# Loading the first head group's q and k in memory order, with 32-row score products, in a fused attention and mixture-of-experts kernel

## The chip, the cores and the metric

The kernel runs on one core of a Trainium2 chip. The metric is the device time of one execution in microseconds (us). Before the change the median of three runs is 844.26 us (844.2 to 844.76). The execution that the profiler recorded took 843.34 us, with a span of 841.6 us from its first to its last instruction.

## The reference

Attention over 8 batches, 12 heads, 448 positions and 64 dimensions per head, with capped scores, followed by a mixture of 8 experts in which tokens are assigned in order of their gate logits. All numbers are float32.

```
scores = q @ k.T / sqrt(64)
scores = cap * tanh(scores / cap)
attn   = softmax(scores);  x = attn @ v        # x: 3584 tokens of 12*64
logits = x @ w_gate;  each token goes to one of 8 experts, 448 tokens each
out    = relu(x @ w1[e]) @ w2[e]
```

## The kernel before

The attention stage takes about the first 300 us, the experts the rest. Attention works on 24 groups of four heads; a group is called g0, g1 and so on. Queries and keys must have the 64 dimensions on partitions, so each group's q and k are turned by VectorE transposes of 32x32 blocks (function `tr`). For that, `load` brings q and k in as `(k s) d -> s k d` with s=32, in runs of 32 floats (128 bytes). After the transposes a head fills 64 partitions, and two heads stand beside each other in the free dimension.

`qk(g,r)` makes part r of seven of a group's scores: 64 keys of each of the four heads against all 448 queries, as four TensorE products of 64 rows by 64 columns that fill the four quarters of the array, into one PSUM tile of two banks (`two_banks`, three tiles in turn: psM and two ps). ScalarE takes the tile out with a Tanh (L166) and applies Exp to two or three parts at once (L171). `avq` (letter A) multiplies the exponentials with v into a further tile of two banks, psA; `esum` (P, C, S) adds the exponentials up on VectorE. In g1 and later the keys of part r are `r:S:7`, every seventh, so that v can be loaded in long runs; g0 takes its keys in blocks instead, and its v in two tiles `nv0` and `nvh`.

The order on every engine is written out by hand (`manual_schedule`): strings of letters such as `EARLY[0]`, which is g0, say in which order Q (scores), A, transposes of the next group (k, v) and `I` stand. `I6` is `idle(6)`: six products of the identity with itself into psA, whose result nobody reads. Loads are issued by SyncE (SP) in program order, in g0 also by ScalarE's queue; each load from SP waits until the load eight places before it has landed. The table `LD` says which loads stand at the start of which of the first groups ('10' is k of g1, '11' its q, '02' v of g0).

So for g0: k and q come in two halves of eight loads each (L90), two transposes follow each half (L140), three parts of scores follow the first half, four the second.

Of the kernel before, what the change touches and what calls it, by code (L numbers as in the profile page):

```python
# [17 lines left out]
def attention(nc, tc, c1, xp, pM, ep, nl, pT, q, k, v, cap, w_gate, xs, L1, ident, on_logits, on_turn, NDEF, setup, mark, ring):  # L18
# [5 lines left out]
    N=B*NQ  # L24
# [23 lines left out]
    with ExitStack() as ctx:  # L48
# [15 lines left out]
        def load(g,part,lo=0,hi=HG,first=False):  # L64
            if g>=N: return
            b,m=divmod(g,NQ)
            h0=4*m
            if part==2:
                if g:
# [6 lines left out]
                z=nat.tile([128,3,2*HG,D],F32,name="nv0",bufs=1); zh=nat.tile([128,HG,D],F32,name="nvh",bufs=1)  # L76
                nats[g,2]=(z,zh)
                vv=v[b,h0:h0+4,0:384].rearrange("h (j p) d -> j p h d",j=3)
                for j in range(3): nc.sync.dma_start(z[:,j],vv[j])
                for o in range(2):  # L80
                    w=64*(1-o)
                    nc.sync.dma_start(zh[w:w+64],v[b,h0+o:h0+o+3:2,384:448].rearrange("t p d -> p t d"))
                return
            if lo==0: nats[g,part]=nat.tile([128,HG*NB,32],F32,name="kq"[part])
            z=nats[g,part]
            src=(k,q)[part]
            for t in range(2):
                for a in range(2):
                    w=(2*t+a)*32
                    (nc.scalar if first and a else nc.sync).dma_start(z[w:w+32,lo*NB:hi*NB,:],src[b,h0+2*t+lo:h0+2*t+hi,:,a*32:a*32+32].rearrange("h (k s) d -> s (h k) d",s=32))  # L90
        for part in range(2): load(0,part,0,1,True)
        tb=c1.tile([128,1],F32,name="tb")
        nc.scalar.activation(tb,ident[:,0:1],AF.Tanh)
        ips=pT.tile([128,2,512],F32,name="psA",bufs=1)[:,0]
        def idle(n):
            for _ in range(n): nc.tensor.matmul(ips[:,:128],ident,ident,start=True,stop=True)  # L96
# [4 lines left out]
        ones=c2.tile([128,5,32],F32,name="ones")  # L101
# [5 lines left out]
        for o in range(2): nc.gpsimd.memset(ones[:,3+o,24+2*o:25+2*o],1.0)  # L107
# [27 lines left out]
        FIRST=[[(2+h,ones,3,(0,0,h),0) for h in range(2)],[gate(0),gate(1)]+[(2+h,ones,4,(0,1,h),0) for h in range(2)],RB,RE]  # L135
        tks={}; es_t={}; eh={}; misc={}
        def tr(g,part,lo=0,hi=HG):
            if g>=N: return
            if lo==0: tks[g,part]=tp.tile([128,HG,S],F32,name="t"+"kq"[part])
            nc.vector.transpose(tks[g,part].rearrange("p m s -> p (m s)")[:,lo*S:hi*S],nats[g,part][:,lo*NB:hi*NB,:].rearrange("p k d -> p (k d)"))  # L140
        GRP=((0,1,2),(3,4),(5,6)); LOC={r:(gi,n) for gi,rs in enumerate(GRP) for n,r in enumerate(rs)}
        def ev(g,r):
            gi,n=LOC[r]
            return eh[g,gi][:,n]
        ex=lambda g,o,j: ev(g,3*o+j)
        wait=[]; G2=3
        def qk(g,r):
# [3 lines left out]
            if g:  # L151
                for o in range(2):
                    for h in range(2):
                        hp=slice(h*64,h*64+64)
                        nc.tensor.matmul(ps[o*64:o*64+64,h,:S],tks[g,0][hp,o,r:S:7],tks[g,1][hp,o,:],start=True,stop=True)  # L155
            elif r<6:
                o,u=divmod(r,3)
                for h in range(2):
                    hp=slice(h*64,h*64+64)
                    for c in range(2): nc.tensor.matmul(ps[c*64:c*64+64,h,:S],tks[g,0][hp,o,u*128+c*64:u*128+c*64+64],tks[g,1][hp,o,:],start=True,stop=True)  # L160
            else:
                for o in range(2):
                    for h in range(2):
                        hp=slice(h*64,h*64+64); w=64*(1-o)
                        nc.tensor.matmul(ps[w:w+64,h,:S],tks[g,0][hp,o,384:448],tks[g,1][hp,o,:],start=True,stop=True)
# [6 lines left out]
            if g==0 or g==N-1 and gi: act()  # L172
            else: wait.append(act)
        def esum(g,what):
            if not 0<=g<N: return
            if what=='P': es_t[g]=es.tile([128,2,2,S],F32,name="es",bufs=4)
            t=es_t[g]; add=lambda o,x,y: nc.vector.tensor_tensor(o,x,y,op=ALU.add)  # L177
            if what=='P':
                if g: add(t,eh[g,0][:,0:2],eh[g,1])
                else:  # L180
                    for o in range(2): add(t[:,o],ev(g,3*o),ev(g,3*o+1))
            elif what=='C': add(t[:,0],t[:,0],ev(g,2))
            elif what=='r': add(t[:,0],t[:,0],t[:,1])
            elif g: add(t,t,eh[g,2])
            else:
                add(t[:,1],t[:,1],ev(g,5))
                e=ev(g,6)
                for o in range(2):
                    w=slice(64*(1-o),128-64*o)
                    add(t[w,o],t[w,o],e[w])  # L190
        avp={}; pair=[None]
        def avq(g,r):
            if not 0<=g<N: return
            if r==0:
# [3 lines left out]
            if g:  # L198
                z=nats[g,2]
                for o in range(2):  # L200
                    hp=slice(o*64,o*64+64)
                    for h in range(2):
                        nc.tensor.matmul(avp[g,o][h*64:h*64+64,:S],z[hp,r,h,:] if g==N-1 else z[hp,h,r*D:r*D+D],ev(g,r)[hp,h,:],start=r==0,stop=r==6)  # L203
                return
            j,x=(r%3,r//3) if r<6 else (3,1)
            z,zh=nats[g,2]
            for w in range(2):
                o=w^x; hp=slice(w*64,w*64+64)
                for h in range(2):
                    lhs,rhs=(z[hp,j,HG*h+o,:],ex(g,o,j)) if j<3 else (zh[hp,h,:],ev(g,6))  # L210
                    nc.tensor.matmul(avp[g,o][h*64:h*64+64,:S],lhs,rhs[hp,h,:],start=(j==0 and x==0),stop=j==3)
# [128 lines left out]
        for part in range(2): load(0,part,1,2)  # L340
        setup[0]()
        setup[1]()
        for part in range(2): tr(0,part,0,1)
# [5 lines left out]
        for a,t in zip(sr,(s1,capt)): nc.scalar.reg_load(a,t[0:1,0:1].bitcast(I32))  # L349
        bias=c1.tile([128,1],F32,name="bias")  # L350
# [3 lines left out]
        for part in range(2): tr(0,part,1,2)  # L354
        LD={0:['10','11','02','20','21'],1:['12','30','31','g','22'],2:['40','41','32','50','51']}
# [4 lines left out]
        EARLY=["Q0 Q1 k v Q2 I6 Q3 Q4 Q5 Q6 I18","Q0 Q1 A0 P C k S v Q2 A1 A2 Q3 Q4 Q5 Q6 A3 A4 A5 A6","Q0 c Q1 A0 P C k v S r Q2 A1 A2 Q3 Q4 A3 Q5 Q6 A4 A5 A6"]  # L360
# [867 lines left out]
```

## Time and profile before

| what | value |
|---|---|
| median of 3 runs | 844.26 us |
| profiled execution | 843.34 us, span 841.6 us |
| TensorE busy | 829.1 us, 99% |
| VectorE / ScalarE / GpSimd busy | 607.4 / 550.4 / 450.0 us |
| attention | about 0 to 300 us |

A busy TensorE is near its limit all the time, so the table alone does not say where a microsecond can be won. The chain of waits follows the work that ended last back from the end; the timeline shows one engine in order of time, with the idle time before an instruction and what ended it.

### The profile page before, as it was taken

What the parts mean: (1) busy time and instruction counts of PE and PEld (TensorE: products, weight loads), DVE (VectorE), ACT (ScalarE), POOL (GpSimd) and SP (SyncE); (2) the same over time, 40 slices, a digit from 0 to 9 for tenths busy, and PEclk for the clock granted to TensorE, in tenths of its full rate; (3) what the DMA queues carried; (4) which work ended last, traced back from release to release, by engine and by line L of the source; (5) the groups of instructions that cost most, each with busy time, mean ns of one, the idle gap of its engine ahead of it and who ended that gap; (6) DMA issues with size and microseconds to landing.
All of it is one profiled execution on the core that took longest, in us unless ns stands there. A gap on an engine that the chain in (4) does not pass through costs nothing.

```text
span 841.6 us, 17561 instructions
## 1 busy us (share of the span) xinstructions
PE 829.1 (99%) x6053; PEld 640.9 (76%) x6053; DVE 607.4 (72%) x1955; ACT 550.4 (65%) x750; POOL 450.0 (53%) x637
## 2 busy tenths in 40 slices
PE   9999999999999998999999999999999999999997
PEld 6444444444444458889999999999999999999997
DVE  3778899989989877777988888878978973221110
ACT  6999999999999754561664655646636635535521
POOL 8303335344332235573683874856857857846931
PEclk9999999999999999999999999999999999999999
DMA  8999999999993206715716926917918828738501
GB/s 120 140 153 157 157 169 162 160 161 167 156 156 83 44 3 208 252 39 170 232 32 175 316 73 196 341 46 212 315 55 217 293 77 234 252 123 255 186 10 57
DMA packets 330457, 133.70 MB, mean 159 GB/s; under 512 B 251168, under 2 KB 323680, under 8 KB 330368
## 3 DMA queue, kind: packets, MB, share of 16 engines
q1 hardware_dynamic: 320864, 102.27, 55.8%
q0 software_dynamic: 4656, 22.02, 7.6%
q10 hardware_dynamic: 4848, 8.29, 2.9%
q8 instruction: 48, 0.79, 0.4%
q14 instruction: 41, 0.34, 0.1%
HBM read 94.40 MB, written 30.08 MB: 148 GB/s over the span
## 4 chain that ended last, share of the span: by engine, by line
PE 87%; DVE 5%; ACT 4%; issue 3%; POOL 1%; POOLq 0%; DVEq 0%
PE psH L1062 28%; PE psH L1096 26%; PE psA L203 12%; PE ps L155 8%; PE psM L155 4%; ACT e L171 2%; ACT e L166 2%; PE ps L228 2%; PE psA L96 1%; DVE cmpD L614 1%; DVE es L177 1%; PE psX L886 1%; PE psM L228 1%; POOL out_dram L1078 0%; PE psR L809 0%
## 5 line engine op out<-in xcount | busy, mean ns | idle before, releaser
L1096 PE MATMUL psH<-w2h,hh 128*128 128x384 f32 x896 | 232.5, 338 | 0.0
L1096 PE MATMUL psH<-w2l,hh 128*128 128x384 f32 x512 | 166.1, 340 | 0.0
L1096 PEld LDWEIGHTS psH<-w2h,hh 128*128 128x128 f32 x896 | 161.9, 188 | 0.1
L171 ACT ACTIVATE e<-e,bias 128x1792 f32<-128x1792 f32 (+2 forms) x73 | 151.3, 2072 | 0.2
L1062 PE MATMUL psH<-xgh,w1h 128*128 128x448 f32 x384 | 141.5, 369 | 0.3 <-ACT xgh L1022 0.3
L1062 PE MATMUL psH<-xgh,w1l 128*128 128x448 f32 x384 | 140.9, 367 | 0.0
L944 POOL TENSOR_TENSOR w1l<-w1r,w1h 128x768 fp32r<-128x768 f32 x62 | 114.3, 1845 | 40.4 <-ACT w1h L940 35.8
L1062 PE MATMUL psH<-xgl,w1h 128*128 128x448 f32 x384 | 135.6, 366 | 0.0
L203 PE MATMUL psA<-e,nv 64*64 64x448 f32 x1232 | 130.7, 539 | 0.6 <-DVE xT L217 0.5
L944 POOL TENSOR_TENSOR w2l<-w2r,w2h 128x768 fp32r<-128x768 f32 x64 | 118.1, 1848 | 3.2 <-ACT w2h L940 3.2
L166 ACT ACTIVATE e<-ps 128x896 f32<-128x896 f32 x113 | 103.9, 961 | 7.7 <-PE ps L155 3.8
L155 PE MATMUL ps<-tq,tk 64*64 64x448 f32 x864 | 97.1, 539 | 0.1
L203 PEld LDWEIGHTS psA<-e,nv 64*64 64x64 f32 x1232 | 45.4, 133 | 67.8 <-issue 61.0
L1096 PEld LDWEIGHTS psH<-w2l,hh 128*128 128x128 f32 x512 | 95.6, 188 | 0.2
L1071 DVE SCALAR_TENSOR_TENSOR hh<-psH,hh 128x64 fp32r<-128x64 f32 (+1 forms) x128 | 44.0, 385 | 65.2 <-ACT hh L1068 65.1
L1068 ACT ACTIVATE hh<-psH 128x448 fp32r<-128x448 f32 x64 | 34.7, 543 | 83.2 <-PE psH L1062 83.1
L1102 ACT ACTIVATE on<-psH 128x384 f32<-128x384 f32 x48 | 23.6, 491 | 84.6 <-PE psH L1096 79.6
L969 POOL DMA_INDIRECT xg<-xs,idx x32 | 34.7, 1086 | 81.7 <-DVE idx L824 55.4
L1062 PEld LDWEIGHTS psH<-xgh,w1h 128*128 128x128 f32 x384 | 72.3, 188 | 6.0 <-ACT xgh L1022 0.5
L1062 PEld LDWEIGHTS psH<-xgl,w1h 128*128 128x128 f32 x384 | 72.2, 188 | 5.5
L1062 PEld LDWEIGHTS psH<-xgh,w1l 128*128 128x128 f32 x384 | 72.2, 188 | 5.5
L177 DVE TENSOR_TENSOR es<-es,e 128x896 f32<-128x896 f32 (+2 forms) x48 | 72.8, 1517 | 4.3 <-ACT e L171 1.5
(417 smaller groups left out, 1409.3 us busy)
## 6 DMA issues: line engine op xcount, KB each, us to landing
w1r<-in_moe_w_dram SPq DMA_DIRECT2D x128, 192.0 KB, 4.8
w2r<-in_moe_w_dram SPq DMA_DIRECT2D x64, 384.0 KB, 6.1
k<-in_k_dram SPq DMA_DIRECT2D x92, 112.0 KB, 3.6
q<-in_q_dram SPq DMA_DIRECT2D x92, 112.0 KB, 4.1
nv<-in_v_dram SPq DMA_DIRECT2D x88, 112.0 KB, 3.0
xs<-xw SPq DMA_DIRECT2D x72, 112.0 KB, 2.6
xz<-pl ACTq DMA_DIRECT2D x18, 384.0 KB, 3.0
xs<-xn SPq DMA_DIRECT2D x1, 1344.0 KB, 6.6
```

The lines of the kernel that those rows point to most:

```text
L155: nc.tensor.matmul(ps[o*64:o*64+64,h,:S],tks[g,0][hp,o,r:S:7],tks[g,1][hp,o,:],start=True,stop=True)
L166: nc.scalar.activation(ev(g,r),ps[:,:,:S],AF.Tanh,scale=sr[0])
L171: act=lambda: nc.scalar.activation(e,e,AF.Exp,scale=sr[1],bias=bias)
L177: t=es_t[g]; add=lambda o,x,y: nc.vector.tensor_tensor(o,x,y,op=ALU.add)
L203: nc.tensor.matmul(avp[g,o][h*64:h*64+64,:S],z[hp,r,h,:] if g==N-1 else z[hp,h,r*D:r*D+D],ev(g,r)[hp,h,:],start=r==0,stop=r==6)
L228: nc.tensor.matmul(bank[b][q*32:q*32+32,:S],t[:,a,:],rhs,start=n==mine[0],stop=n==mine[-1])
L944: (eng or nc.gpsimd).tensor_tensor(view(l),r,view(h).bitcast(F32),op=ALU.subtract)
L969: g=nc.gpsimd.indirect_dma_start(out=row(j,n),out_offset=None,in_=xs,in_offset=bass.IndirectOffsetOnAxis(ap=res[p][0][:n,j:j+1],axis=0))
L1062: nc.tensor.matmul(ps[:,:C],a[:,c,:],b[:,c,:],start=(m==0),stop=(m==DC*3-1)); m+=1
L1068: nc.scalar.activation(h[:,:C],ps[:,:C],AF.Relu)
L1071: nc.vector.scalar_tensor_tensor(h[:,d:d+b-a],ps[:,a:b],0.0,h[:,a:b].bitcast(F32),op0=ALU.max,op1=ALU.subtract)
L1096: nc.tensor.matmul(ps[:,:HD],h[:,f,a:a+128],spl[p,2,hf,f//2][w][:,f%2,:],start=(m==0),stop=(m==nm-1))
```

## The change

Only g0 changes its way of working; the loads, transposes and sums of other groups keep theirs.

- **Loads** (`load0`). k and q of g0 are read as they lie in memory: partition (head, s) holds 14 consecutive positions with all 64 dimensions, 3584 bytes. There are four loads in place of sixteen: the keys of parts 0 and 1, and q's second half, on SP's queue; q's first half and the remaining keys on ScalarE's.
- **Transposes** (`tr0`). Six in place of four: two of 128 elements per partition for the keys of parts 0 and 1 (written 8 bytes apart), two of 448 for q's halves, two of 320 for the other keys.
- **Scores** (`qk0`). After these transposes a head stands on 32 partitions, and its dimensions in two halves. A score part is the sum of two products of 32 rows by 64 columns. Two parts run together into two tiles, 16 products in all, with parts 1, 4 and 6 (`SWAP`) in the other half of the output partitions, so that eight tiles of the array have work at once. Parts 0 and 1 come in two halves of 224 queries; their fourth tile is psA. The queries are read as `s k` with k innermost: neighbours lie 64 floats (256 bytes) apart.
- **v twice.** g0's v is loaded as that of other groups (nv), and a second time with the head pairs on exchanged partitions (nvx) for the swapped parts; nv0 and nvh are gone.
- **Order.** Fewer idle products at the start (9, not 13), and J8, I10, I8 in place of I6 and I18. Part 2 comes last. A takes g0's parts in the order 1 4 6 0 2 3 5.

```
+        def load0(eng,part,lo,hi,two=False):
+            src=(k,q)[part][0,0:4].rearrange("h (s k) d -> (h s) (k d)",s=32)
+            if two: eng.dma_start(halfs(z)[:,:,lo:hi],halfs(src)[:,:,lo:hi])
+            else: eng.dma_start(z[:,lo:hi],src[:,lo:hi])
...
-        for part in range(2): load(0,part,0,1,True)
-        idle(13)
+        load0(nc.sync,0,0,128,True)
+        load0(nc.scalar,1,0,448)
         nc.sync.dma_start(capt,cap.broadcast_to([128,1]))
+        load0(nc.sync,1,448,896)
+        load0(nc.scalar,0,128,448,True)
+        idle(9,True)
...
+                z=nats[g,3]=nat.tile([128,HG,7*D],F32,name="nvx",bufs=1)
+                    for t in range(2): nc.sync.dma_start(z[64-o*64:128-o*64,t],v[b,h0+2*t+o].rearrange("(p j) d -> p (j d)",j=7))
...
+        def qk0(rs,cuts=(0,14)):
+            tk=tks[0,0].rearrange("p a (j x) -> p j a x",j=7)
+            tq=tks[0,1].rearrange("p m s -> p (m s)").rearrange("p (k a s) -> p a s k",a=2,s=32)
+            for lo,hi in zip(cuts,cuts[1:]):
+                W=(hi-lo)*32
+                ts=[(r,pT.tile([128,2,512],F32,name="psA",bufs=1) if lo and r==rs[-1] else two_banks()) for r in rs]
+                for a in range(2):
+                    for n in range(4):
+                        h,o=divmod(n,2); hp=slice(n*32,n*32+32)
+                        for r,ps in ts:
+                            w=64*(1-o if r in SWAP else o)
+                            nc.tensor.matmul(ps[w:w+64,h,:W].rearrange("p (s k) -> p s k",s=32),tk[hp,r,a],tq[hp,a,:,lo:hi],start=a==0,stop=a==1)
+                for r,ps in ts: nc.scalar.activation(ev(0,r).rearrange(...)[:,:,:,lo:hi],ps[:,:,:W].rearrange(...),AF.Tanh,scale=sr[0])
+            nc.scalar.activation(e,e,AF.Exp,scale=sr[1],bias=bias)
...
-        for part in range(2): tr(0,part,0,1)
+        tr0(0,0,2)
         nc.vector.reciprocal(rcap,capt)
+        tr0(1,0,448); tr0(1,448,896)
-        for part in range(2): tr(0,part,1,2)
+        tr0(0,2,7)
-        LD={0:['10','11','02','20','21'],1:['12','30','31','g','22'],2:['40','41','32','50','51']}
+        LD={0:['10','11','02','03','20','21'],1:['12','30','31','g','22'],2:['40','41','32','50','51']}
-        EARLY=["Q0 Q1 k v Q2 I6 Q3 Q4 Q5 Q6 I18","Q0 Q1 A0 P C k S v Q2 A1 A2 Q3 Q4 Q5 Q6 A3 A4 A5 A6",...]
+        EARLY=["Q01/7 k v Q34 J8 Q56 I10 Q2 I8","Q0 Q1 A1 P C k S v Q2 A4 A6 Q3 Q4 Q5 Q6 A0 A2 A3 A5",...]
```

TensorE's order in g0, before (64x448 is output partitions by queries; x4 says four in a row; L96 is the idle product, L160 and L165 scores of g0, L155 scores of g1):

```order
L96 MATMUL psA<-ident 128x128 x13
L160 MATMUL ps_397<-tq,tk 64x448 x4
L160 MATMUL ps_403<-tq,tk 64x448 x4
L160 MATMUL psM<-tq,tk 64x448 x4
L96 MATMUL psA<-ident 128x128 x6
...
L165 MATMUL ps_447<-tq,tk 64x448 x4
L96 MATMUL psA<-ident 128x128 x18
L155 MATMUL ps_513<-tq,tk 64x448 x4
```

And after (L105 is the idle product, L176 scores of g0, L188 scores of g1, L218 the products with v; parts that run together alternate between two tiles):

```order
L105 MATMUL psA<-ident 128x128 x9
L176 MATMUL ps_386<-tq,tk 64x224
L176 MATMUL ps_387<-tq,tk 64x224
...
L105 MATMUL psA<-ident 128x128 x8
L176 MATMUL psM<-tq,tk 64x448
L176 MATMUL ps_464<-tq,tk 64x448
...
L105 MATMUL psA<-ident 128x128 x10
L176 MATMUL ps_494<-tq,tk 64x448 x8
L105 MATMUL psA<-ident 128x128 x8
L188 MATMUL psM<-tq,tk 64x448 x4
L188 MATMUL ps_560<-tq,tk 64x448 x4
L218 MATMUL psA<-e_385,nvx 64x448 x4
```

Behind the first scores stand 24 idle products before (6 and 18) and 26 now (8, 10 and 8); ahead of them 13 before and 9 now. Every pair of parts takes sixteen products.

VectorE's start, before and after (tk and tq are the turned k and q, L140 before and L152, L154, L147 after):

```order
L452 TENSOR_SCALAR r_qi<-r_qi 128x32
L140 STREAM_TRANSPOSE tk<-k 128x448
L140 STREAM_TRANSPOSE tq<-q 128x448
L345 RECIPROCAL rcap<-capt 128x1
L347 TENSOR_SCALAR s_359<-rcap 128x1
L351 TENSOR_SCALAR bias<-capt 128x1
```

```order
L460 TENSOR_SCALAR r_qi<-r_qi 128x32
L152 STREAM_TRANSPOSE tk<-k 128x2x2x32 x2
L351 RECIPROCAL rcap<-capt 128x1
L353 TENSOR_SCALAR s_342<-rcap 128x1
L154 STREAM_TRANSPOSE tq<-q 128x448 x2
L358 TENSOR_SCALAR bias<-capt 128x1
L359 TENSOR_TENSOR bias<-bias,capt 128x1
L360 TENSOR_SCALAR bias<-bias 128x1
L152 STREAM_TRANSPOSE tk<-k 128x5x2x32 x2
```

The scale (rcap and the instruction after it) now stands ahead of q's transposes, and the transposes of the remaining keys behind the bias.

SyncE's loads, before and after (k and q of 32x14x32 are halves of g0; 32x28x32 are those of g1):

```order
L90 DMA k<-in_k_dram 32x14x32 x2
L90 DMA q<-in_q_dram 32x14x32 x2
L100 DMA capt<-in_cap_dram 128x1
L90 DMA k<-in_k_dram 32x14x32 x4
L90 DMA q<-in_q_dram 32x14x32 x4
L90 DMA k<-in_k_dram 32x28x32 x4
L90 DMA q<-in_q_dram 32x28x32 x4
```

```order
L69 DMA k<-in_k_dram 128x2x128
L97 DMA capt<-in_cap_dram 128x1
L70 DMA q<-in_q_dram 128x448
L93 DMA k<-in_k_dram 32x28x32 x4
L93 DMA q<-in_q_dram 32x28x32 x4
L81 DMA nv<-in_v_dram 64x448 x4
L85 DMA nvx<-in_v_dram 64x448 x4
```

The loads of g1's k and q move from places 14 to 21 of SP's queue to places 4 to 11.

## Rows read from the trace of the kernel before

**Rows 1.** The page: busy times, clock in 40 slices, the chain's shares by engine.
```profile
PE 829.1 (99%) x6053; PEld 640.9 (76%) x6053; DVE 607.4 (72%) x1955; ACT 550.4 (65%) x750; POOL 450.0 (53%) x637
...
PEclk9999999999999999999999999999999999999999
...
PE 87%; DVE 5%; ACT 4%; issue 3%; POOL 1%; POOLq 0%; DVEq 0%
```

**Rows 2.** The chain that ended last, 0 to 60 us: start, duration, what.
```profile
1.50 5.47 PE psA L96 x26
6.97 0.96 PE ps L160 x8
...
14.89 4.21 PE psA L96 x36
19.10 1.00 PE ps L155 x8
20.10 0.75 PE psM L155 x8
...
24.67 0.92 ACT e L166
...
52.49 1.04 PE ps L155 x8
```

**Rows 3.** VectorE's timeline, start-up: start, duration, what, and idle before.
```profile
4.11 0.31 DVE L452 TENSOR_SCALAR r_qi<-r_qi 128x32 int32<-128x32 int32 x1
4.79 0.65 DVE L140 STREAM_TRANSPOSE tk<-k 128x448 f32<-128x448 f32 x1 [0.37 <-DMA k<-in_k_dram]
5.88 0.65 DVE L140 STREAM_TRANSPOSE tq<-q 128x448 f32<-128x448 f32 x1 [0.44 <-DMA q<-in_q_dram]
6.45 0.12 DVE L345 RECIPROCAL rcap<-capt 128x1 f32<-128x1 f32 x1
...
6.67 0.14 DVE L351 TENSOR_SCALAR bias<-capt 128x1 f32<-128x1 f32 x1
...
17.80 1.11 DVE L140 STREAM_TRANSPOSE tq<-q 128x896 f32<-128x896 f32 x1 [2.62 <-DMA q<-in_q_dram]
```

**Rows 4.** ScalarE's timeline, 7 to 25 us.
```profile
7.95 1.73 ACT L166 ACTIVATE e<-ps 128x896 f32<-128x896 f32 x2 [3.62 <-PE ps L160]
...
10.52 2.54 ACT L171 ACTIVATE e<-e,bias 128x2688 f32<-128x2688 f32 x1
...
16.39 0.90 ACT L166 ACTIVATE e<-psM 128x896 f32<-128x896 f32 x1
...
18.12 1.79 ACT L171 ACTIVATE e<-e,bias 128x1792 f32<-128x1792 f32 x1
20.16 0.92 ACT L166 ACTIVATE e<-ps 128x896 f32<-128x896 f32 x1 [0.25 <-PE ps L155]
```

**Rows 5.** L96's products, 1 to 5 us, then 16 to 18 us: min/median/max.
```profile
L96 PE MATMUL psA<-ident x16: 421/421/582, 1.5 to 4.9; 128*128 128x128 f32 x16
...
L96 PE MATMUL psA<-ident x20: 275/275/275, 15.8 to 17.9; 128*128 128x128 f32 x20
```

**Rows 6.** Issues on SP's queue: start, time in issue, what.
```profile
8.24 2.29 SPq L90 DMA_DIRECT2D k<-in_k_dram  x4
10.57 3.23 SPq L90 DMA_DIRECT2D q<-in_q_dram  x4
```

**Rows 7.** DMA issues, 0 to 30 us: count, KB each, median us to landing.
```profile
nv<-in_v_dram SPq DMA_DIRECT2D x4, 112.0 KB, 3.8
...
q<-in_q_dram ACTq DMA_DIRECT2D x2, 56.0 KB, 3.4
```

**Rows 8.** Weight loads by line: ns min/median/max, first and last start, form.
```profile
L155 PEld LDWEIGHTS ps<-tq,tk x136: 187/191/215, 21.0 to 59.4; 64*64 64x64 f32 x136
...
L203 PEld LDWEIGHTS psA<-e,nv x144: 129/133/133, 31.1 to 57.9; 64*64 64x64 f32 x144
...
L228 PEld LDWEIGHTS ps<-es,ones x72: 106/110/110, 60.2 to 293.7; 128*32 128x32 f32 x72
```

More of the change, by code (lines that the diff above doesn't have):

```diff
@@ L63, in attention, with load @@
         nats={}
-        def load(g,part,lo=0,hi=HG,first=False):
+        halfs=lambda t: t.rearrange("p (c x) -> p c x",c=2)
+        def load0(eng,part,lo,hi,two=False):
+            if (0,part) not in nats: nats[0,part]=nat.tile([128,HG*NB,32],F32,name="kq"[part])
+            z=nats[0,part].rearrange("p k d -> p (k d)")
+            src=(k,q)[part][0,0:4].rearrange("h (s k) d -> (h s) (k d)",s=32)
+            if two: eng.dma_start(halfs(z)[:,:,lo:hi],halfs(src)[:,:,lo:hi])
+            else: eng.dma_start(z[:,lo:hi],src[:,lo:hi])
+        def load(g,part,lo=0,hi=HG):
             if g>=N: return
@@ L89, in load, with idle @@
                     w=(2*t+a)*32
-                    (nc.scalar if first and a else nc.sync).dma_start(z[w:w+32,lo*NB:hi*NB,:],src[b,h0+2*t+lo:h0+2*t+hi,:,a*32:a*32+32].rearrange("h (k s) d -> s (h k) d",s=32))
-        for part in range(2): load(0,part,0,1,True)
[L92 to L96, printed above, removed]
-        idle(13)
+                    nc.sync.dma_start(z[w:w+32,lo*NB:hi*NB,:],src[b,h0+2*t+lo:h0+2*t+hi,:,a*32:a*32+32].rearrange("h (k s) d -> s (h k) d",s=32))
+        load0(nc.sync,0,0,128,True)
+        load0(nc.scalar,1,0,448)
         capt=c1.tile([128,1],F32,name="capt")
         nc.sync.dma_start(capt,cap.broadcast_to([128,1]))
-        ones=c2.tile([128,5,32],F32,name="ones")
+        load0(nc.sync,1,448,896)
+        tb=c1.tile([128,1],F32,name="tb")
+        load0(nc.scalar,0,128,448,True)
+        nc.scalar.activation(tb,ident[:,0:1],AF.Tanh)
+        ips=[]
+        def idle(n,new=False):
+            if new: ips[:]=[pT.tile([128,2,512],F32,name="psA",bufs=1)[:,0]]
+            for _ in range(n): nc.tensor.matmul(ips[0][:,:128],ident,ident,start=True,stop=True)
+        idle(9,True)
+        ones=c2.tile([128,4,32],F32,name="ones")
         nc.gpsimd.memset(ones,0.0)
@@ L140, in tr, with tr0 @@
             nc.vector.transpose(tks[g,part].rearrange("p m s -> p (m s)")[:,lo*S:hi*S],nats[g,part][:,lo*NB:hi*NB,:].rearrange("p k d -> p (k d)"))
+        def tr0(part,lo,hi):
+            if (0,part) not in tks: tks[0,part]=tp.tile([128,HG,S],F32,name="t"+"kq"[part])
+            if part==0:
+                for c in range(2):
+                    nc.vector.transpose(tks[0,0].rearrange("p a (j s c) -> p c j a s",j=7,c=2)[:,c,lo:hi],nats[0,0].rearrange("p (c j a) d -> p c j a d",c=2,j=7)[:,c,lo:hi])
+                return
+            nc.vector.transpose(tks[0,part].rearrange("p m s -> p (m s)")[:,lo:hi],nats[0,part].rearrange("p k d -> p (k d)")[:,lo:hi])
+        SWAP=(1,4,6); AO=((1,4,6,0,2,3,5),range(7))
         GRP=((0,1,2),(3,4),(5,6)); LOC={r:(gi,n) for gi,rs in enumerate(GRP) for n,r in enumerate(rs)}
@@ L146, in attention @@
         wait=[]; G2=3
+        def qk0(rs,cuts=(0,14)):
+            for r in rs:
+                gi,n=LOC[r]
+                if (0,gi) not in eh: eh[0,gi]=ep.tile([128,len(GRP[gi]),2,S],F32,name=f"e{gi}")
+            tk=tks[0,0].rearrange("p a (j x) -> p j a x",j=7)
[9 more added lines that the diff above has]
+                            nc.tensor.matmul(ps[w:w+64,h,:W].rearrange("p (s k) -> p s k",s=32),tk[hp,r,a],tq[hp,a,:,lo:hi],start=a==0,stop=a==1)
+                for r,ps in ts: nc.scalar.activation(ev(0,r).rearrange("p h (s k) -> p h s k",k=14)[:,:,:,lo:hi],ps[:,:,:W].rearrange("p h (s k) -> p h s k",s=32),AF.Tanh,scale=sr[0])
+            gi,n=LOC[rs[0]]
+            e=eh[0,gi][:,n:n+len(rs)]
+            nc.scalar.activation(e,e,AF.Exp,scale=sr[1],bias=bias)
         def qk(g,r):
@@ L150, in qk @@
             ps=two_banks()
[L151 to L157, printed above, removed]
+            for o in range(2):
                 for h in range(2):
                     hp=slice(h*64,h*64+64)
[L160 to L165, printed above, removed]
+                    nc.tensor.matmul(ps[o*64:o*64+64,h,:S],tks[g,0][hp,o,r:S:7],tks[g,1][hp,o,:],start=True,stop=True)
             nc.scalar.activation(ev(g,r),ps[:,:,:S],AF.Tanh,scale=sr[0])
@@ L178, in esum @@
             if what=='P':
-                if g: add(t,eh[g,0][:,0:2],eh[g,1])
-                else:
-                    for o in range(2): add(t[:,o],ev(g,3*o),ev(g,3*o+1))
+                add(t,eh[g,0][:,0:2],eh[g,1])
             elif what=='C': add(t[:,0],t[:,0],ev(g,2))
             elif what=='r': add(t[:,0],t[:,0],t[:,1])
[L184 to L190, printed above, removed]
+            else: add(t,t,eh[g,2])
         avp={}; pair=[None]
@@ L197, in avq @@
                 pair[0]=two
[L198 to L208, printed above, removed]
+            x=g==0 and r in SWAP
+            z=nats[g,2+x]
+            for o in range(2):
+                w=o^x; hp=slice(w*64,w*64+64)
                 for h in range(2):
-                    lhs,rhs=(z[hp,j,HG*h+o,:],ex(g,o,j)) if j<3 else (zh[hp,h,:],ev(g,6))
-                    nc.tensor.matmul(avp[g,o][h*64:h*64+64,:S],lhs,rhs[hp,h,:],start=(j==0 and x==0),stop=j==3)
+                    nc.tensor.matmul(avp[g,o][h*64:h*64+64,:S],z[hp,r,h,:] if g==N-1 else z[hp,h,r*D:r*D+D],ev(g,r)[hp,h,:],start=r==AO[g>0][0],stop=r==AO[g>0][6])
         def av_out(g):
```

26 lines of the change are left out of this document (10 added, 16 removed).

## The prediction

> **What bounds the kernel now.** I read the busy times first: TensorE is busy 99% of the span, and the chain of waits is TensorE for 87% [rows 1]. A start-up change can therefore pay only by letting TensorE reach the long stretch sooner. So the chain of waits over the first 60 us came next [rows 2]. The reader is to see two hand-overs in it. The first scores of g0 start at 6.97, behind 26 passes of idle products (13 products, two passes each). The first scores of g1 start at 19.10, behind 36 such passes (I18). From there TensorE's rounds run until ScalarE takes over at 24.67, ScalarE carries the chain to 52.49, and TensorE from then on. A round is what fills the array once: 0.75 us for one part of scores [rows 2].
>
> VectorE's timeline shows what stood behind the second hand-over besides the idle products [rows 3]: g1's q is turned only at 17.80 to 18.91, after 2.62 us of waiting for its load. 18.91 to 19.10 is the time from a transpose to the product, 0.19 us. ScalarE works through g0 from 7.95 to 19.91 (18.12 + 1.79) and gets g1's first tile at 20.16 [rows 4]. Three engines thus reach the border between g0 and g1 within half a microsecond of each other: loads with VectorE, TensorE by its idle products, ScalarE. Removing one of them alone gains little. What decides is when TensorE starts g1's first scores (now 19.10), because the rest of the chain hangs on it.
>
> **The loads.** Before, q of g1 was issued at 10.57 to 13.80 [rows 6], behind twenty other loads. Now its four loads are eighth to eleventh on SP's queue, ahead of v. The rate of issue in these rows is 0.57 to 0.81 us per load, so eleven loads are issued by about 8 us, and with 3.4 to 3.8 us to land (the values shown for loads of this size and half of it [rows 7]) g1's q is in VectorE's hands at about 12, nearly 6 us sooner. That wait goes, and what is late next is TensorE's own order. v doubled adds 448 KB in four loads; nv and nvx are issued after q by about 8 x 0.8 = 6.4 us, at 14.5, and are in by 18.3 with 3.8 us to land [rows 7]. Their first reader, A1, comes two rounds after g1's first scores, at about 20.6. They are hidden by 2 us; beyond that each microsecond of lateness would be paid in full.
>
> For g0 the first transposes waited for loads of 56 KB: k's landed for a transpose at 4.79, q's for 5.88 [rows 3]. Now the first load from each queue must land, 128 KB and 224 KB in long runs. No row shows these. Bounds: as quickly as the 56 KB loads (3.4 us, 4.2 on the clock), or later by the additional bytes, some 1 us (5.2). In both cases VectorE's order is the later: it is busy with constants until 4.42 (4.11 + 0.31).
>
> **The start of the scores.** A transpose of 448 takes 0.65 and of 896 1.11 [rows 3], so 0.19 + 0.46 per 448 elements: 0.32 for 128, 0.52 for 320. VectorE: 4.42 + 2 x 0.32 (keys of parts 0 and 1) + 0.22 for the scale (6.45 to 6.67) + 0.65 (q's first half) = 5.93. TensorE starts at 5.93 + 0.19 = 6.1, not 6.97. The nine idle products (18 passes of 0.21, from 1.50) end at 5.3, so they are not in the way. Writing the keys 8 bytes apart has no row; between nothing and a doubling of the four key transposes (1.7 us in all, 0.6 of it before the first scores) I take nothing, since later slack eats part of it.
>
> **TensorE through g0.** Likeliest is that sixteen products of 32 rows cost what eight of 64 rows cost: eight tiles at once fill the array as four quarters do, so a pair of parts is two rounds, 1.50 us, and part 2 alone two rounds as well (its second product must follow on the same tile). That makes 8 rounds, 6.0 us, in place of 7, 5.25. Idle passes cost 4.21 / 36 = 0.117 each [rows 2]: J8 1.87, I10 2.34, I8 1.87, in all 6.1 against 5.6. Step by step:
> - parts 0 and 1: 6.1 to 7.6.
> - parts 3 and 4 need the other keys: VectorE 5.93 + 0.65 (q's second half) + 0.5 (three small bias operations, 0.14 busy and some 0.17 apart) + 2 x 0.52 = 8.1, TensorE 8.3 to 9.8. This is 0.7 us of waiting.
> - J8 to 11.7. Parts 5 and 6 need the tile of part 3 back from ScalarE. ScalarE's first Tanh starts 0.98 after the product (7.95 against 6.97), so at 7.1; four half Tanhs of about 0.5 and an Exp of 1.79 later it is 10.9, and 11.8 after part 3's Tanh. So 11.8 to 13.3.
> - I10 to 15.7, part 2 to 17.2, I8 to 19.0.
>
> So g1's first scores start at 19.0, 0.1 before the 19.10 of now. VectorE's operations follow each other a little closer than I summed, which may give 0.1 to 0.2 more; I take 0.2 in all.
>
> **ScalarE through g0.** It has two Tanhs and one Exp more for the same elements. An Exp of 2688 takes 2.54 and one of 1792 1.79, so 0.75 per 896 elements; what is left over is 0.29 per Exp and 0.15 per Tanh [rows 4]. The addition is at most 0.29 + 2 x 0.15 = 0.6. From 7.1, 12.0 + 0.6 brings it to 19.7, before the 20.0 at which g1's first tile is ready (19.0 + 0.98). It does not bind, but by 0.3 only. Writing 7 of 14 queries at a time has no row; it would have to cost more than 0.3 in four instructions to be felt.
>
> **What lies beside.** g0's sums on VectorE lose some instructions (seven additions become three); VectorE is not on the chain there, so nothing is counted. From g2 on every queue holds the same instructions, with the three PSUM tiles one place further in their turn. Sum: the profiled execution of 843.34 becomes 843.1; the median of the runs shown lies 0.92 above that execution, so 844.0.
>
> **A rule against it.** Weight loads of 64 columns take 133 ns when the columns adjoin (L203) and 191 when they lie 28 bytes apart (L155); 32 adjoining take 110 [rows 8]. An adjoining column costs (133 - 110) / 32 = 0.7 ns and a spread one 0.9 ns more. The new scores read their queries 256 bytes apart, and no row shows a product that streams its moving operand so. [...] I take the unspread 0.75 because the bound that the nearest product row gives is for adjoining columns, and keep the other as a rival.
>
> **Rival 1: the rounds take double.** If a query read 256 bytes apart costs 0.9 ns more, a round of two passes over 448 gains 896 x 0.9 = 0.8 us. Eight rounds make 6.4; 0.8 of it disappears in the two waits above (0.7 and 0.1), so g1 starts 5.6 later and the time is 849.6, slower. It decides the sign from 0.3 us more per round on (8 x 0.3 less 0.8 is 1.6). For it: the weight loads, and that no strided product has a row. Against: a product's pass takes twice as long per column as the weight load needs, 0.75 us for 896 columns or 0.84 ns each beside 0.7, and could have a fetch to spare. The same price comes about if only four of the eight tiles run at once. Heads n=0 and n=1 write the two halves of one bank from different rows of the array; in g1 each bank is written from one half of the rows. [...] I give the two together 0.20.
>
> **Rival 2: the first scores run at the lower clock.** Idle products took 421 ns at first and 275 later [rows 5], with a granted clock shown as full in every slice [rows 1]; the change shortens the first block and leaves TensorE 0.8 us idle before the scores. [...] 0.10.
>
> **Rival 3: more is gained.** ScalarE idles 0.25 us before g1's first tile [rows 4] and somewhat more until 24.67; if the two waits in g0 vanish, TensorE's sum is 6.1 + 6.0 + 6.1 = 18.2 and 0.9 is gained: 843.3. Beyond that the idle products would have to be shorter than their rows, or the relief of the loads would have to reach further than g1; if ScalarE's idle time up to 24.67 went too, 842. 0.14, of which 0.12 for this further reach; against it that TensorE's order is fixed. **Rival 4: v's second copy is late.** If nvx lands 4 us later than summed, A1 holds g1 by 2: 846. 0.04.
>
> **How the numbers follow.** The forecast itself has 0.52, with 843.3 to 845.0 as its own range. A measurement of this kernel tells 0.2% (1.7 us) from no change. Faster than 842.6 needs the further reach of rival 3: 0.12. Slower than 845.9 comes from rival 1 with 0.19 (0.01 for a partial cost that stays below) and rival 4 with 0.03: 0.22. No change has the rest, 0.66. The range goes from 842.3 to 848.5, which leaves out the full rival 1 in most of its cases and the far end of rival 3, about 2 in 10.
>
> **What would show it.** Right: g1's first scores between 18.7 and 19.3, the pair of parts 3 and 4 in about 1.5 us, VectorE turning g1's q by 13 without a wait after it. Rival 1: pairs of about 3 us and part 2 alone 3 (or, if banks are the cause, part 2 too, though it has four tiles). [...] The prediction is wrong if g1's first scores move by more than 1.7 us, or if they stay and the end moves.

## The result: 1.0% slower

The changed kernel takes 852.74 us (median of 5 runs, 851.92 to 853.45) where the kernel before takes 844.2 in the same series (843.66 to 844.76). The ratio is 1.010, with a 95% interval of 1.0088 to 1.0111. The forecast was 844.0, its range ended at 848.5: both were too low. Over all series the kernel before has a median of 844.05 (21 runs).

The page of the profile, to be read against [rows 1]:

```profile
span 851.0 us, 17716 instructions
...
PE 837.2 (98%) x6137; PEld 641.9 (75%) x6137; DVE 607.7 (71%) x1954; ACT 552.0 (65%) x753; POOL 445.6 (52%) x637
...
PE 82%; DVE 6%; issue 3%; ACT 3%; DMA 3%; SPq 1%; POOL 0%; POOLq 0%; DVEq 0%
```

TensorE is busy for 8.1 us more (837.2 against 829.1) though it makes the same scores. The chain of waits shows where, against [rows 2] (start, duration, what):

```profile
1.48 4.68 DMA capt<-in_cap_dram
...
7.13 2.16 PE ps L176 x28
...
11.06 3.59 PE ps L176 x32
14.64 1.98 PE psA L105 x16
...
20.72 2.43 PE psA L105 x20
23.14 3.16 PE ps L176 x16
26.30 1.98 PE psA L105 x16
28.29 0.97 PE psM L188 x8
```

The second group's first scores (L188) start at 28.29; they started at 19.10. These 9.2 us are the whole loss: the span grew by 9.4. They lie in the first group's scores (L176). Parts 5 and 6 run from 16.62 (14.64 + 1.98) to 20.72, which is 4.10 us for a pair summed at 1.50; part 2 takes 3.16, also summed at 1.50. ScalarE, which had worked through g0 almost without a stop [rows 4], now waits for them (the last column is the idle time before an instruction and what ended it):

```profile
9.35 1.08 ACT L177 ACTIVATE e<-ps 128x448 f32<-128x448 f32 x2 [5.96 <-PE ps L176]
...
20.84 0.92 ACT L177 ACTIVATE e<-psM 128x896 f32<-128x896 f32 x1 [2.52 <-PE ps L176]
```

The loads and VectorE come later than summed too. VectorE's timeline, against [rows 3]:

```profile
4.33 0.49 DVE L152 STREAM_TRANSPOSE tk<-k 128x128 f32<-128x128 f32 x2
6.18 0.16 DVE L351 RECIPROCAL rcap<-capt 128x1 f32<-128x1 f32 x1 [1.35 <-DMA capt<-in_cap_dram]
...
6.44 0.64 DVE L154 STREAM_TRANSPOSE tq<-q 128x448 f32<-128x448 f32 x1
8.11 0.65 DVE L154 STREAM_TRANSPOSE tq<-q 128x448 f32<-128x448 f32 x1 [1.03 <-DMA q<-in_q_dram]
...
9.20 0.90 DVE L152 STREAM_TRANSPOSE tk<-k 128x320 f32<-128x320 f32 x2
```

The first transpose of q stands in program order behind the cap's reciprocal, and that waits for a load of half a kilobyte until 6.18. The granted clock also fell, which the 40 slices of the page are too coarse to show. In stretches (busy time of TensorE, granted clock, DMA share, GB/s):

```profile
7.50:8.00 0.50, 0.50 (x16) 1.00 0.98 87
8.00:8.50 0.50, 0.50 (x16) 0.53 1.03 138
8.50:9.00 0.50, 0.50 (x18) 0.50 0.96 117
...
11.00:11.50 0.50, 0.50 (x15) 0.56 1.05 147
```

The granted clock falls from 1.00 to 0.50 here, behind 1.91 us in which TensorE stood still (its idle time before the products of 7.13). So three causes offer themselves: the spread reading of the queries (theory A), late loads, and the lower clock (theory C from the section on the clock on; in the first two expectations C stands for "half of each"). A further candidate is that eight tiles of 32 rows, or two writing one bank, do not run at once.

### The profile page after: what moved, and what is told of

It reads as the page before. It is cut to its first block, busy times and chain, and to the rows that moved or that the text cites. A ratio compares the mean times of both kernels' runs of the same rounds, so it can differ in the third digit from the quotient of the medians.

```text
span 851.0 us, 17716 instructions
## 1 busy us (share of the span) xinstructions
PE 837.2 (98%) x6137; PEld 641.9 (75%) x6137; DVE 607.7 (71%) x1954; ACT 552.0 (65%) x753; POOL 445.6 (52%) x637
## 4 chain that ended last, share of the span: by engine, by line
PE 82%; DVE 6%; issue 3%; ACT 3%; DMA 3%; SPq 1%; POOL 0%; POOLq 0%; DVEq 0%
PE psH L1070 28%; PE psH L1104 26%; PE psA L218 10%; PE ps L188 6%; PE psM L188 3%; DVE es L200 2%; ACT e L194 2%; ACT e L189 1%; PE ps L235 1%; DMA q<-in_q_dram 1%; DVE cmpD L622 1%; PE ps L176 1%; SPq L93 1%; PE psA L105 1%; PE psX L894 1%
## 5 line engine op out<-in xcount | busy, mean ns | idle before, releaser
L194 ACT ACTIVATE e<-e,bias 128x1792 f32<-128x1792 f32 (+2 forms) x70 | 145.2, 2074 | 0.1
L218 PE MATMUL psA<-e,nv 64*64 64x448 f32 x1264 | 133.9, 539 | 0.6 <-DVE xT L224 0.5
L189 ACT ACTIVATE e<-ps 128x896 f32<-128x896 f32 x107 | 98.6, 966 | 2.9 <-PE ps L188 2.8
L218 PEld LDWEIGHTS psA<-e,nv 64*64 64x64 f32 x1264 | 46.5, 133 | 69.8 <-issue 62.8
L188 PE MATMUL ps<-tq,tk 64*64 64x448 f32 x856 | 95.4, 538 | 0.0
L200 DVE TENSOR_TENSOR es<-es,e 128x896 f32<-128x896 f32 (+1 forms) x46 | 71.6, 1556 | 11.9 <-ACT e L180 8.0
```

## The experiments

All numbers below that stand alone are of one run; "g1" is the start of the second group's first scores, in the execution that the profiler recorded. A block is what streams at once: eight passes of 32-row products for a pair of parts, four for part 2; a pair or a part has four blocks.

**Spread reading.** First, two adjoining queries, then a step of 256 bytes (the output order of g0's queries differs):

```
-  tq=...rearrange("p (k a s) -> p a s k",a=2,s=32)
+  tq=...rearrange("p (k a s i) -> p a s k i",a=2,i=2,k=14)
```

> The changed kernel with g0's query columns streamed in another order: two neighbouring queries (8 bytes) side by side, then a step of 256 bytes; g0's queries therefore come out in another order, so this run is read for its durations alone. In the changed kernel a pair of parts takes 4.0 us in four blocks of 0.95 (eight tiles at once), part 2 alone 3.15 in four blocks of 0.79 (four tiles at once). Theory A (each column read 256 bytes from its neighbour costs a fetch of its own; two in one line hide it): blocks fall to about 0.38 to 0.45, a pair to 1.5 to 1.8 us, part 2 to 1.5, g1's first scores from 28.3 to about 21, the time to about 846. Theory B (products of 32 rows, or eight tiles and two writers to one bank, are slow whatever the order of the columns): blocks stay at 0.95 and 0.79, the time at 852.7. Theory C (half of each): part 2 falls to 1.5 to 1.6, the pair only to about 2 to 2.5.

Measured: 846.61 us, g1 at 21.73. Then four adjoining queries (i=4):

> As the run with two neighbours, but four neighbouring queries (16 bytes) side by side; again g0's queries come out in another order and only durations are read. Theory A: if two neighbours are enough to hide the fetch, this is the same as with two (pair 1.5 to 1.8 us, part 2 1.5); if the cost falls with the number of fetches, blocks go 0.95, then about 0.6 with two, then 0.4 with four. Theory B: 0.95 and 0.79 as before, 852.7 us. Theory C: as with two.

Measured: 846.37 us, g1 at 21.43. The chain of the first of them, then of the second:

```profile
11.60 1.98 PE psA L105 x16
...
15.64 2.43 PE psA L105 x20
18.07 1.68 PE ps L176 x16
```

```profile
11.69 1.98 PE psA L105 x16
...
15.36 2.43 PE psA L105 x20
17.79 1.66 PE ps L176 x16
```

Parts 5 and 6 fill what lies between the two idle blocks: 2.06 us (13.58 to 15.64) and 1.69 (13.67 to 15.36), against 4.10. Part 2 takes 1.68 and 1.66, against 3.16. Products, weights, tiles and banks are those of the changed kernel, so they are not the cause by themselves. Only the distance between columns differs. 6.1 of the 8.5 us are back with two adjoining columns. With two, the pair's 2.06 lies above theory A's 1.5 to 1.8 and where "half of each" put it (2 to 2.5); with four it is 1.69, which leaves nothing to the tiles. So two neighbours are enough for four tiles and not quite for eight.

Third, with the reference's output, VectorE's transposes write the queries in the order in which they are read, so that the products read 448 adjoining columns:

```
+  nc.vector.transpose(tks[0,part].rearrange("p a (s k) -> p k a s",s=32)[:,lo//64:hi//64],
+                      nats[0,part].rearrange("p (k a) d -> p k a d",a=2)[:,lo//64:hi//64])
```

> The changed kernel, but VectorE's transposes put g0's queries down in the order in which TensorE reads them (writing 56 bytes apart), so the products stream adjoining columns (runs of 7 for the two halves, 448 adjoining for the other parts). Theory A: the pair of parts 3 and 4 takes 1.5 us instead of 4.0, part 2 1.5 instead of 3.15, and since the loads and VectorE's order stay (first scores at 7.1, other keys turned by 10.1), g1's first scores start near 20.9: 28.3 - 20.9 = 7.4 less, so 852.7 - 7.4 = 845.3, still 1 above the kernel before. If writing 56 bytes apart slows VectorE's transposes of 448 from 0.65 to 1.3, the first scores come 0.65 later. Theory B: 4.0 and 3.15 stay, 852.7.

Measured: 847.35 us, ratio 1.0031 (1.0017 to 1.0045), g1 at 22.68. Parts 3 and 4 take 1.50 in the chain, just what the prediction summed:

```profile
11.02 1.50 PE ps L176 x32
```

But the parts before did not speed up: their halves take 1.80 and 1.76, and each transpose of q takes 0.93 to 0.96 instead of 0.64.

The same doubling can be made in the kernel before. There g0's four 64-row products per round were given queries 256 bytes apart:

```
-  ...ps[c*64:c*64+64,h,:S],...,tks[g,1][hp,o,:],
+  ...rearrange("p (s k) -> p s k",k=7),...,tks[g,1][hp,o,:].rearrange("p (k s) -> p s k",k=7),
```

> The kernel before, with one edit: the first group's queries are streamed with 256 bytes from one column to the next (its queries come out in another order, so the first group's output is not the reference's). Products, rows, weights, loads and waits stay those of before. [...] Rival (it is the 32-row tiles, or two of them in one bank, that made the changed kernel's rounds long): 64-row products do not mind, the round stays 0.75 and the time 844.2.

Measured: 849.48 us, g1 at 25.31. The chain, where [rows 2] has rounds of 0.75:

```profile
11.03 1.52 PE psM L160 x8
12.55 1.53 PE psA L96 x12
...
17.98 1.59 PE psM L160 x8
19.58 1.51 PE ps L165 x8
```

The rounds that stand alone in the chain go from 0.75 to between 1.51 and 1.59; two blocks of part 2 in the changed kernel make 2 x 3.16 / 4 = 1.58. On both kernels the time goes with the distance between columns, as theory A has it, and the 32-row tiles are out as a cause; the fetch and the line that theory A names are in no view. With one, two and four adjoining columns, four tiles took 3.16, 1.68 and 1.66 for part 2, and eight took 4.10, 2.06 and 1.69 for parts 5 and 6. Every column that stands alone in these products lies 256 bytes from the next; a smaller step for such columns was not tried, so at which distance a product begins to take longer is not measured here.

**The loads.** The cap's load was moved to the front of SP's queue:

```
+  nc.sync.dma_start(capt,cap.broadcast_to([128,1]))
   load0(nc.sync,0,0,128,True)
```

> The changed kernel with one thing moved: the load of the cap (0.5 KB) is issued first on SyncE's queue, ahead of the keys. In the changed kernel it landed 4.7 us after its issue, and VectorE waited 1.35 us for it ahead of the scale and q's transposes. Theory A: VectorE's scale starts near 4.9 and not at 6.18, the first scores near 6.0 and not at 7.13; q's second half still lands only for 8.1, so the second halves of parts 0 and 1 start no earlier than 8.8 and g1's first scores gain at most 0.3: 852.4. Rival: the start is what the change loses, and the whole 1.1 us comes through to g1 (27.2) and the end, 851.6.

Measured: 853.46 us, g1 at 28.46. Both expectations missed: now the keys come late.

```profile
6.02 0.51 DVE L152 STREAM_TRANSPOSE tk<-k 128x128 f32<-128x128 f32 x2 [1.61 <-DMA k<-in_k_dram]
```

Whichever of the two is issued second is there at 6.0 to 6.2, be it 0.5 KB or 128 KB: for these two the place on the queue sets it, not the cap. Swapping them moves the wait to another reader. In this run q's second half and the other keys were turned a microsecond sooner (other keys at 8.17 instead of 9.20), and g1's start did not move forward: behind products this slow, earlier data is of no use.

**The clock.** Turned queries once more, with TensorE kept at work ahead of the first scores:

```
-        idle(9,True)
+        idle(13,True)
```

> The changed kernel with queries turned into the order of reading, and 13 idle products ahead of the first scores instead of 9. In the run with 9 the blocks of the first parts' halves took 0.37 us where those of parts 3 and 4 took 0.19 us for as many columns (0.38 for 448), after 1.9 us in which TensorE stood still. Theory C (TensorE was slow because it had stood still): with 13 idle products it stands still for less than 1 us, the halves take 0.8 to 1.0 us each instead of 1.8, the second group's first scores come at about 21.9 instead of 22.7, 846.6 us. Rival (reading seven adjoining columns and leaving out seven is slow by itself): halves still 1.8 us, 847.3 us.

Measured: 845.89 us, g1 at 21.59. TensorE's timeline with 9 and with 13 idle products (start, duration, what, idle time before):

```profile
7.56 1.80 PE L176 MATMUL ps<-tq,tk 32*64 32x224 f32 x32 [1.89 <-DVE tq L154]
```

```profile
7.26 1.02 PE L176 MATMUL ps<-tq,tk 32*64 32x224 f32 x32 [0.44 <-DVE tq L154]
```

The same 32 records, read the same way, take 1.02 instead of 1.80: theory C holds for adjoining columns. (The clock column reads 1.00 in both runs; the last section comes back to that.) Is it also a part of the changed kernel's loss? The changed kernel as it is, with 13 idle products:

> The changed kernel as it is, with 13 idle products ahead of the first scores instead of 9. In the changed kernel the granted clock was 0.50 from 8.2 to 11.2 us, behind 1.9 us in which TensorE stood still. With 13 it should stay 1.00, as it did with turned queries. Theory A (the products of the changed kernel are paced by the fetch of their spread columns, whatever the clock): the halves take as long as before, 1.6 to 1.9 us each, parts 3 and 4 3.8 to 4.0, and the time is 852.4 us. Rival (part of the loss is the low clock): the halves take 1.0 to 1.2 us each, and the time falls by as much as it did with turned queries, to 851.2.

Measured: 852.54 us, g1 at 27.97. Stretches and chain:

```profile
8.00:9.00 1.00, 1.00 (x30) 1.00 1.30 134
9.00:10.00 1.00, 1.00 (x32) 1.00 1.28 137
```

```profile
7.17 2.08 PE ps L176 x27
...
10.94 3.50 PE ps L176 x30
```

With a granted clock of 1.00 from 4 to 14 us, the first parts still take until 10.5, as before (10.57), and parts 3 and 4 take 3.95 instead of 4.07. With columns this far apart the time goes with the columns, not with the clock (1.63 us for the second halves at 0.50, 1.56 here at 1.00); the low clock cost the changed kernel nothing that can be told. It is a cost in the runs with adjoining columns: with it over most of their time, parts 3 and 4 took 2.86 and 2.33 (the next two runs) instead of 1.50.

**The order on VectorE.** With turned queries and 9 idle products, q's first half is transposed ahead of the cap's reciprocal:

```
-        tr0(0,0,2)
+        tr0(0,0,2); tr0(1,0,448)
```

> The changed kernel with queries turned into the order of reading, 9 idle products, and the first half of the queries turned ahead of the cap's reciprocal instead of behind it: VectorE need not wait for the cap to land (6.3 us). The first scores should start at 5.8 instead of 7.6, right behind the idle products. Theory C: the first halves then take 0.8 to 1.0 us instead of 1.8, and the second halves, behind more than 2 us in which TensorE stands still, 1.5 to 1.8. Rival (seven adjoining columns are slow by themselves): 1.5 to 1.8 for both. By both the second halves still wait for the second half of the queries (8.3 us), so the second group's first scores move by 0.3 us at most: 847.0 us.

Measured: 848.19 us, g1 at 22.90. The first scores start at 5.71, 1.85 earlier, and take 1.05; then TensorE stands still 2.06 us for q's second half, and the clock falls:

```profile
8.00:9.00 1.00, 0.18 (x8) 1.00 1.14 132
9.00:10.00 1.00, 1.00 (x32) 0.62 1.20 141
10.00:11.00 1.00, 1.00 (x16) 0.50 1.14 138
11.00:12.00 1.00, 1.00 (x24) 0.50 1.18 146
```

Theory C's pattern held (fast first, slow after the gap), but 847.0 was too low: parts 3 and 4 fell into the slow stretch too and took 2.86 instead of 1.50. Here the first scores started 1.85 earlier, then paused, and g1 came 0.2 later (22.90 against 22.68).

**Reading in order without turning.** The queries are streamed as VectorE leaves them, 32 adjoining, and ScalarE's Tanh reads the bank 128 bytes apart:

```
-  tq=...("p (k a s) -> p a s k",...)   ps[...]("p (s k) -> p s k",s=32)   Tanh: ps ("p h (s k) -> p h s k",s=32)
+  tq=...("p (k a s) -> p a k s",...)   ps[...]("p (k s) -> p k s",s=32)   Tanh: ps ("p h (k s) -> p h s k",s=32)
```

> The changed kernel with the queries streamed as VectorE leaves them, 32 adjoining columns, and ScalarE's Tanh reading the scores from their bank 128 bytes apart, so that its result lies as before. Output as the reference. Theory A: parts 3 and 4 1.5 us, part 2 1.7 us, and the transposes stay 0.64 us (they were 0.93 with the queries turned into the order of reading), so first scores at 7.1 instead of 7.6. If ScalarE reads spread columns at its usual rate (0.91 us for 896), the second group's first scores come at about 22.0 and the time is 846.6 us. Rival: a spread read on ScalarE costs as VectorE's spread write did (0.93 against 0.64, so 1.3 us for 896): ScalarE is the engine that the first group waits for, seven parts at 0.4 us more, 849.4 us.

Measured: 847.53 us (846.36 to 847.94), ratio 1.0038 (1.0024 to 1.0052), g1 at 22.27. ScalarE's spread reading costs nothing more: 0.90 and 0.91 us for 896 elements, as before.

```profile
17.28 0.91 ACT L177 ACTIVATE e<-ps 128x896 f32<-128x896 f32 x1
```

The transposes stay at 0.63 to 0.65. The execution that the profiler recorded met the expectation nearly (g1 at 22.27 for 22.0, 846.36 us for 846.6); it is the fastest of the five, and no trace shows where the median's 1.2 us more lie. In it the clock is 0.50 from 8.4 to 11.7 us behind 1.80 us of standing still, and parts 3 and 4 take 2.33 in the chain.

**The idle products on the path.** With 13 idle products and turned queries, ScalarE waited 0.96 us for g1's first scores, which stood behind I8:

```
-  "Q01/7 k v Q34 J8 Q56 I10 Q2 I8"
+  "Q01/7 k v Q34 J8 Q56 I10 Q2 I2"
```

> The run with 13 idle products and turned queries (845.9 us), with the eight idle products behind part 2 cut to two. There ScalarE stood still for 0.96 us ahead of the second group's first scores, which stood behind those idle products on TensorE. Theory D (idle products that cover a wait for ScalarE are on the path where they end later than ScalarE does): the second group's first scores start 1.0 to 1.5 us earlier, at 20.1 to 20.6 instead of 21.6, ScalarE goes from the Exp of part 2 to their Tanh without a stop, and the time is 844.9 us. Rival: TensorE, without those products, is granted the low clock there, or the second group's products wait for something else (its queries, a bank): no gain, 845.9.

Measured: 844.65 us, g1 at 20.25 (19.54 + 0.71 in TensorE's timeline). ScalarE with I8, then with I2:

```profile
20.62 1.04 ACT L180 ACTIVATE e<-e,bias 128x896 f32<-128x896 f32 x1
22.63 0.92 ACT L189 ACTIVATE e<-psM 128x896 f32<-128x896 f32 x1 [0.96 <-PE psM L188]
```

```profile
20.63 1.04 ACT L180 ACTIVATE e<-e,bias 128x896 f32<-128x896 f32 x1
21.57 0.90 ACT L189 ACTIVATE e<-psM 128x896 f32<-128x896 f32 x1
```

Theory D holds: the wait is gone, g1 comes 1.34 earlier, and the time is 1.2 us less (two single runs).

**All together.** 32 adjoining queries with Tanh restoring the order, 13 idle products, q ahead of the reciprocal, I2:

> All that helped, in one kernel with the reference's output: queries streamed as VectorE leaves them with ScalarE's Tanh restoring their order, 13 idle products ahead of the first scores, the first half of the queries turned ahead of the cap's reciprocal, and two idle products behind part 2 instead of eight. First scores at 6.9 (behind the idle products), the second halves at 8.4, the granted clock 1.00 throughout. If ScalarE is what the first group waits for (it is busy without a stop for some 11 us from the second halves on), the second group's first scores come at 19.8 to 20.1 and the time is 844.3 us, what the kernel before takes (19.1 there, with a shorter run of scores ahead of ScalarE). Rival: the low clock comes back in the gap between the halves, as in the run with the reordered transposes: 846.0.

Measured: 844.7 us (843.91 to 845.7, 11 runs), ratio 1.0007 (0.9998 to 1.0016): no difference from the kernel before that can be told. g1 starts 0.65 later than there. Its chain:

```profile
2.10 5.44 DMA q<-in_q_dram
...
7.56 0.65 DVE tq L154
...
9.58 1.76 PE ps L176 x32
11.35 1.98 PE psA L105 x16
...
15.02 2.43 PE psA L105 x20
17.45 1.66 PE ps L176 x16
19.11 0.64 PE psA L105 x4
19.75 0.97 PE psM L188 x8
```

It hangs on the load of q's second half. ScalarE, from 9.37 on, stops nowhere until 22.8; then it waits for g1's third and fourth tile, 0.27 and 1.34 us:

```profile
25.30 0.92 ACT L189 ACTIVATE e<-psM 128x896 f32<-128x896 f32 x1 [1.34 <-PE psM L188]
```

So it is not ScalarE that g1 waits for here. From 9.58 to 25.30 the chain is TensorE's, and 5.05 us of it are idle products (1.98, 2.43 and 0.64). No run made J8 or I10 shorter in this version, so whether it could have won is open. The last try put the load of q's second half ahead of the cap's:

> The same, with the load of the second half of the queries issued ahead of that of the cap. The queries' half landed at 7.7 us with its issue third on its queue; if it is the place in the queue that makes it late, it lands at 7.2, the second halves of scores start at 7.9 right behind the first, and the time is 0.4 us less than without: 843.9. Rival (all the loads share what the DMA engines move, so that the half lands no earlier, and the cap, now third, lands at 6.8 or later): the same time, 844.3, or, if ScalarE's scale is then late, up to 0.5 more.

Measured: 845.2 us (844.76 to 845.78, 11 runs), ratio 1.0016 (1.0007 to 1.0025). The half, now second and issued at 1.47, was in hand when VectorE came to it at 8.12, behind the scale; whether it landed before the 7.54 of the run before is not shown. The cap, now third, is waited for until 7.85 (6.20 when it was second), so the order counts for it, and ScalarE's first Tanh starts at 9.17 instead of 8.13. That is the rival's loss.

How g1's start carries the time, over the runs, each with the time of the execution that the profiler recorded:

| run | g1 starts, us | time of that execution, us | difference |
|---|---|---|---|
| before | 19.10 | 843.34 | 824.24 |
| all together | 19.75 | 845.70 | 825.95 |
| I2 | 20.25 | 844.65 | 824.40 |
| cap third | 20.42 | 845.66 | 825.24 |
| four adjoining | 21.43 | 846.37 | 824.94 |
| 13 idle, turned | 21.59 | 845.89 | 824.30 |
| two adjoining | 21.73 | 846.61 | 824.88 |
| 32 adjoining | 22.27 | 846.36 | 824.09 |
| turned | 22.68 | 847.68 | 825.00 |
| q ahead of the reciprocal | 22.90 | 848.19 | 825.29 |
| before, spread | 25.31 | 849.48 | 824.17 |
| changed, 13 idle | 27.97 | 852.54 | 824.57 |
| changed | 28.29 | 852.74 | 824.45 |
| cap first | 28.46 | 853.46 | 825.00 |

The difference stays within 1.9 us over 9 us of g1's start, and executions of the kernel before differ by as much among themselves (842.98 to 845.16). The chain carries the start without that noise. TensorE takes it back from ScalarE at 52.49 before [rows 2] and here in the changed kernel:

```profile
61.67 1.04 PE psM L188 x8
```

From g1's start that is 33.39 and 33.38 us, and it is 33.36 to 33.39 in the nine executions whose chain shows it. What decides a start-up change here is that one start.

## Why the prediction was wrong

**Right.** The prediction named the one quantity that decides, g1's first scores, and the table bears it out. Keys written 8 bytes apart cost nothing (0.49 for the two transposes, 0.64 summed). Eight tiles did work at once, with two row tiles writing one bank (each its own half of the partitions): 1.50 to 1.76 for the pair when columns adjoin and the granted clock is 1.00. That settles the second half of rival 1 (four of eight tiles, or one bank): it did not happen. Rival 4 did not happen either: no instruction waited for v's second copy (issued from 14.2 to 16.1 us, 2.8 to 2.9 to land, first read at 29.8).

**The step that failed** is "sixteen products of 32 rows cost what eight of 64 rows cost": 8 rounds at 0.75, 6.0 us. The spread reading was seen, and sized in rival 1 at 0.8 us per round from weight loads 28 bytes apart, with a chance of 0.20. The cause was named, and 0.8 was right for four tiles: part 2 has (3.16 - 1.50) / 2 = 0.83. With eight tiles it is (4.10 - 1.50) / 2 = 1.30; why it is more with eight than with four is not shown. All rounds together gained 1.94 + 2.57 + 2.60 + 1.66 = 8.8 us: parts 0 and 1 took 3.44 (7.13 to 10.57), parts 3 and 4 4.07 (10.57 to 14.64). The two waits of 0.8 that the sum had were filled, as rival 1 said. With a start 1.0 later and some 0.3 for idle blocks this is 19.0 + 8.8 - 0.8 + 1.0 + 0.3 = 28.3, the measured start. A small part of the 8.8 is not the spread: with adjoining columns too, parts 3 and 4, 5 and 6, and 2 took 1.76, 1.69 and 1.66 in the version with everything together, 0.6 more than summed.

The choice behind the step is the instructive one. The nearest row for a product was of adjoining columns, and the nearest row for a spread read was of weight loads; the text took the first as likeliest, and held against the second that "a product's pass takes twice as long per column as the weight load needs". The numbers beside those words, 0.84 ns and 0.7, are not a factor of two, so that time to spare was never in the rows. A column 256 bytes from the next cost 3.16 / 4 / 448 = 1.76 ns with four tiles, which is 0.16 more than the weight loads' 0.7 + 0.9 = 1.6. Reading the weight-load row as a full price per column, and not as an excess to be hidden, would have given 1.6 ns against the 0.84 of a pass: rounds of 1.43, and the slower side as the likeliest.

**Loads.** First scores at 6.1 were summed, 7.13 came. VectorE was summed as the later of the two; it was the cap's load, 4.68 us in the chain, which the sum did not have. q's second half was turned at 8.11, summed at 5.93. g1's q was to be in hand at 12 and was turned at 15.03, because k's four loads took 4.76 us to issue instead of some 3; nothing waited for it. (Of the "twenty other loads" that it stood behind before, seventeen were on its own queue.)

```profile
2.64 4.76 SPq L93 DMA_DIRECT2D k<-in_k_dram  x4
```

**ScalarE.** "At most 0.6" more: its instructions in g0 add up to 13.05 us in the version with everything together and to 12.29 before, 0.76 more. It is hidden in the changed kernel, whose ScalarE waits for TensorE. In the version with everything together ScalarE reaches g1's first tile 0.91 later than before (21.07 against 20.16), but it waits for TensorE again after two tiles; what keeps that version from winning is TensorE's start of g1, 0.65 later.

**Rival 2** (lower clock) happened: the granted clock was 0.50 from 8.0 to 11.4 us. It cost nothing that can be told: from the second halves to parts 3 and 4 it took 1.63 us at 0.50 (8.94 to 10.57) and 1.56 at 1.00 in the run with 13 idle products.

## What to carry to other kernels

Look at the innermost step of a product's moving operand before anything else: 256 bytes doubled a round of four tiles (0.75 to 1.51) and made a pair on eight 2.4 times as long (4.10 against 1.69), while two adjoining columns already brought back most of it. Put the new order on the side that reads or writes it for nothing, here ScalarE's read of the scores (0.91 either way), not VectorE's write (0.93 against 0.64). In a start-up, follow one quantity, the start of the first long stretch, and check for each idle product and each small operation whether it stands ahead of it in program order. A filler sized for one order of work may be too long for the next.

## What was not expected of the hardware

- A spread read on ScalarE from a bank (128 bytes apart) took 0.90 to 0.91 us for 896 elements, as an adjoining one; a spread write of VectorE's transpose (56 bytes apart) took 0.90 to 0.96 instead of 0.64 for 448, and one 8 bytes apart took 0.49 for two of 128, less than the 0.64 that was summed for adjoining ones.
- The granted clock fell to 0.50 behind standstills of 1.80 (32 adjoining), 1.91 (changed) and 2.06 us (q ahead of the reciprocal) and stayed at 1.00 behind 1.89 (turned), 1.84 (the cap third) and 1.71 (two adjoining). Why it stayed there is open.
- With turned queries and 9 idle products the column shows 1.00 from 7 to 11 us, yet products took 0.37 us per block of 224 columns where 0.19 is usual, as in the runs at 0.50. A clock column at 1.00 is no proof of full pace; the duration of the products is. The idle products of the start say the same [rows 5].
